# Seven block products for half of the up tiles, two unit queues merged by readiness, and loads without staging copies

## The chip, the core and the metric

The kernel runs on one core of one Trainium2 chip. The metric is the device time in microseconds (us) of one execution. Before the change it took 415.5 us (median of 4 runs, 415.48 to 416.22). A core has TensorE (the matmul engine, PE in the profile; PEld is its weight loads), VectorE (DVE), ScalarE (ACT), GpSimd (POOL) and SyncE (SP), which each take their instructions in order, and DMA queues that move data.

The kernel is built by a program that keeps a **plan**: for every instruction it works out when it would start and end, from fixed durations, and it orders the instructions of all engines by these times. The plan prints nothing, but its times can be read while it orders. They are its own estimates and not measurements. Below, "the plan ends at 408.2" is such a time, and "drift" is the start of a matmul in the trace minus its start in the plan. "Before" and "after" are used as the names of the two kernels.

## The reference, cut to what matters

```python
batch, n_q_heads, n_kv_heads, seq, head_dim = (8, 16, 4, 384, 64)
n_tokens, d_model, d_ff = (3072, 1024, 2048)

def reference(q, k, v, w_in, w_out):
    scores = matmul(q, k.T) / sqrt(64)          # 4 query heads share one kv head
    o = matmul(softmax(scores), v)
    x = o.transpose(0, 2, 1, 3).reshape(3072, 1024)
    h = maximum(x @ w_in, 0.0)                  # "up": 1024 -> 2048, then squared
    return (h * h) @ w_out                      # "down": 2048 -> 1024
```

Each batch gives 384 tokens. For one batch, up is 16 tiles of 128 columns of d_ff by 384 tokens. Down is already done in 2x2 blocks by 7 products in place of 8 (sums of operands before, sums of results after) in both kernels.

## The kernel before

Nearly every matmul is cut into pieces of 64 rows of the contraction. Two such pieces run side by side in the two halves (row groups) of the array. Both halves of a unit add into the same PSUM bank, so the second half may start only when the first is through. The plan's clock, with its two constants:

```python
SEM = 60.0       # an end is seen by another instruction 60 ns later
DRAIN = 190.0    # a matmul's result is there 190 ns after its columns

def add(self, eng, fn, reads, writes, ..., ns, rows, end):
    t = max([self.idle_at[eng]] + [self.ops[d]["end"] + self.SEM for d in need])
    if eng == "tensor":
        groups = (0, 1) if rows is None else (rows,)
        free = max([self.idle_at[eng]] + [self.rows_at[x] for x in groups])
        t = max(t, free)
        self.idle_at[eng] = t
        for x in groups:
            self.rows_at[x] = t + ns
        done = t + ns + self.DRAIN
    ...
```

The second half of a unit is held back, in row group 1 always, by a fixed 450 ns from the start of the last piece of its first half:

```python
GAP = 450.0
def hold_back(hi, last, done, frees=()):
    job = dict(hi=list(hi), ready=R.ops[last]["start"] + GAP, after=[last], ...)
    behind.append(job)
```

One up tile is 8 + 8 pieces of 384 columns; an attend unit (softmax weights by v) is 18 + 18 pieces of 65 columns:

```python
def row_up(b, c, then=None, final=False):
    i = yield from next_bank()
    def piece(h, kc):
        rows = ROWS[h]
        return Piece(h, 162.5, lambda pe: pe.matmul(acc[:, 0:S],
            w_in_sb[rows, kc, c * 128:(c + 1) * 128], xT[b % NXT][rows, kc, :], ...))
    def done():          # VectorE: relu out of PSUM; then ScalarE: square
        ...
    lo, hi = ([piece(h, kc) for kc in range(NKC)] for h in range(2))
    yield from push("up", lo, hi, done)
```

Keys and values of the next batch come into staging tiles by rows of 3 x 64 elements, and GpSimd copies them into place:

```python
def load_k(b, after=(), end=None):
    R.add("gpsimd", lambda g: g.dma_start(k_st..., k[b].rearrange("g (p j) d -> p g (j d)", j=NJ)), ...)
def dup_all_k(b, eng="vector"):      # each key twice, side by side
    R.add(eng, lambda e: e.tensor_copy(k_dup[1][:, :, :, :], src.to_broadcast([128, HKV * NJ, 2, D])), ...)
```

The softmax here doesn't subtract the row's maximum and nothing guards it: scores larger than these inputs give would overflow.

Of the kernel before, what the change touches and what calls it, by code (L numbers as in the profile page):

```python
# [9 lines left out]
class Recorder:  # L10
# [6 lines left out]
    def __init__(self, nc):  # L17
        self.nc = nc
        self.ops = []
        self.writer = {}  # L20
        self.readers = {}
        self.dma_sems = {}
        self.dma_last = {}
        self.idle_at = dict.fromkeys(self.ENGINES, 0.0)
        self.rows_at = [0.0, 0.0]
        self.stalled = {}
# [3 lines left out]

    def needs(self, eng, reads, writes, dma=None, after=()):
        deps = set()
# [9 lines left out]
        for d in deps:  # L42
            o = self.ops[d]
            if o["dma"] is None and o["eng"] == eng and dma is None:
                if eng in self.IN_ORDER or d not in raw:
                    continue
            need.add(d)
# [5 lines left out]
    def add(self, eng, fn, reads=(), writes=(), dma=None, after=(), ns=500.0, lat=2200.0, rows=None, end=None):  # L53
        i = len(self.ops)
        need = self.needs(eng, reads, writes, dma, after)
# [81 lines left out]
def bass_gqa_attention__then__ffn_squared_relu_kernel(  # L137
# [23 lines left out]
    NEX, NXT, NHR, NY, NO, NS = 3, 3, 3, 6, 4, 5  # L161

    R = Recorder(nc)

# [4 lines left out]
    warm = sb("warm", [128, 256])  # L169
# [10 lines left out]
    k_st = sb("k_st", [128, HKV, NJ, D])  # L180
    v_st = sb("v_st", [128, HKV, NJ, D])
    k_dup = [a_late[:, 0:2 * NKV].rearrange("p (a x d) -> p a x d", a=HKV * NJ, x=2), sb("k_dup1", [128, HKV * NJ, 2, D]).ap()]
    EARLY_W = [("q_f", c) for c in range(NPB)] + [("k_f", g) for g in range(HKV)] + ["v_f"] + [("q_st", 0, c) for c in range(NPB)]
    EARLY_A = [("k_dup", 0, g, j) for g in range(HKV) for j in range(NJ)]
    q_st = [q_b0, q_next.ap()]
    v_aug = [sb(f"v_aug{i}", [128, HKV * NJ, D + 1]) for i in range(2)]
    kT = [sb(f"kT{i}", [128, HKV, S]) for i in range(2)]
    qT = [sb(f"qT{i}", [128, NPB, S]) for i in range(2)]
    expT = [sb(f"expT{i}", [128, 2 * NJ, S]) for i in range(NEX)]
    rinv = [sb(f"rinv{i}", [128, NJ, 2], f32) for i in range(2)]  # L190
    o_sb = [sb(f"o_sb{i}", [128, NJ, 2, D]) for i in range(NO)]
    xT = [sb(f"xT{i}", [128, NKC, S]) for i in range(NXT)]
    w_in_sb = sb("w_in_sb", [128, NKC, FF], f16)
    w_out_sb = sb("w_out_sb", [128, NFC, F], f16)
    hr = [sb(f"hr{i}", [128, S], f32) for i in range(NHR)]
    h2T = [sb(f"h2T{i}", [128, NFC, S]) for i in range(2)]
    y_sb = [sb(f"y_sb{i}", [128, F // 2], f32) for i in range(NY)]

# [8 lines left out]
    def load_k(b, after=(), end=None):  # L207
        R.add("gpsimd", lambda g: g.dma_start(
            k_st.ap().rearrange("p g j d -> p g (j d)"),
            k[b].rearrange("g (p j) d -> p g (j d)", j=NJ)),  # L210
            writes=["k_st"], dma="k", after=after, ns=900.0, lat=LOADS, end=end)

    def load_v(b, after=(), end=None):
        R.add("gpsimd", lambda g: g.dma_start(
            v_st.ap().rearrange("p g j d -> p g (j d)"),
            v[b].rearrange("g (p j) d -> p g (j d)", j=NJ)),
            writes=["v_st"], dma="v", after=after, ns=900.0, lat=LOADS, end=end)
# [9 lines left out]
    def load_w_in(i):  # L227
# [3 lines left out]
            writes=[("w_in", i)], dma=f"wi{i}", end=20500.0 + 2700.0 * i)  # L231
# [13 lines left out]
    def first_q(c0, c1):  # L245
# [14 lines left out]
    R.add("vector", lambda e: e.memset(warm[:], 0.0), writes=["warm"])  # L260
# [3 lines left out]
        pattern=[[-1, 128]], channel_multiplier=1), reads=["ident"], writes=["ident"])  # L264
    for i in range(2):
        R.add("gpsimd", lambda e, i=i: e.memset(v_aug[i][:, :, D:D + 1], 1.0), writes=[("v_one", i)])
# [5 lines left out]
    def dup_k(g, eng, j0=0, j1=NJ):  # L272
        src = k_f[:, g, j0:j1].unsqueeze(2).to_broadcast([128, j1 - j0, 2, D])
        R.add(eng, lambda e: e.tensor_copy(k_dup[0][:, g * NJ + j0:g * NJ + j1], src),
              reads=[("k_f", g)], writes=[("k_dup", 0, g, j) for j in range(j0, j1)])
# [43 lines left out]
    def turn_bank(banks):  # L319
        i = banks[slots[0] % len(banks)]  # L320
        slots[0] += 1
        if i >= 5:
            return f_ps[i - 5].ap().bitcast(bf16)[:, 0:S], ("f_ps", i - 5)
        return sc_bf[:, i, 0:S], ("sc", i)

    def turn_on_pe(src, src_keys, dst, dst_keys, banks, eng="vector", n=NJ):
        ps, key = turn_bank(banks)

        def tr(pe):
            for t in range(n):  # L330
                m = pe.matmul(ps[:, t * 128:(t + 1) * 128], src[:, t * 128:(t + 1) * 128], ident[:],  # L331
# [3 lines left out]
        R.add("tensor", tr, reads=[*src_keys, "ident"], writes=[key])  # L335
# [4 lines left out]

    def first_kT(g, b=0, banks=RING, j0=0, j1=NJ):
        turn_on_pe(k_dup[b][:, g * NJ + j0:g * NJ + j1].rearrange("p a x d -> p (a x d)"),
                   [("k_dup", b, g, j) for j in range(j0, j1)], kT[b][:, g, j0 * 128:j1 * 128],
                   [("kT", b, g, j) for j in range(j0, j1)], banks, n=j1 - j0)

    def first_qT(c, b=0, banks=RING):
        turn_on_pe(q_st[b][:, 2 * c:2 * c + 2, :].rearrange("p h e -> p (h e)"), [("q_st", min(b, 1), c)],
                   qT[b][:, c], [("qT", b, c)], banks)

    def first_oT(c, banks=RING, eng="vector"):  # L350
        turn_on_pe(o_sb[c % NO].ap().rearrange("p i s d -> p (i s d)"), [("o_sb", c % NO, x) for x in range(2)],
                   xT[0][:, c], [("xT", 0, c)], banks, eng)

    def dup_all_k(b, eng="vector"):
        src = k_st.ap().rearrange("p g j d -> p (g j) d").unsqueeze(2)
        R.add(eng, lambda e: e.tensor_copy(
            k_dup[1][:, :, :, :], src.to_broadcast([128, HKV * NJ, 2, D])),
            reads=["k_st"], writes=[("k_dup", 1, g, j) for g in range(HKV) for j in range(NJ)], ns=1500.0)

    def turn_k(b, g):  # L360
        gs = slice(g * NJ, (g + 2) * NJ)
        R.add("sync", lambda e: e.dma_start_transpose(
            kT[b % 2][:, g:g + 2].rearrange("p g (j c) -> p (g j) c", j=NJ),
            k_dup[1][:, gs].rearrange("p a x d -> p (a x d)")),
            reads=[("k_dup", 1, x, j) for x in (g, g + 1) for j in range(NJ)],
            writes=[("kT", b % 2, x, j) for x in (g, g + 1) for j in range(NJ)], dma=f"kt{b % 2}_{g}", ns=1250.0)

    def turn_q(b, c):
        cs = (c, c + 1)
        R.add("sync", lambda e: e.dma_start_transpose(  # L370
            qT[b % 2][:, c:c + 2, :].rearrange("p h (t c) -> p (h t) c", t=NJ),
            q_st[1][:, 2 * c:2 * c + 4, :].rearrange("p h e -> p (h e)")),
            reads=[("q_st", 1, x) for x in cs], writes=[("qT", b % 2, x) for x in cs],
# [9 lines left out]
    def prepare_v(b):  # L383
        R.add("gpsimd" if b > 1 else "vector", lambda e: e.tensor_copy(
            v_aug[b % 2][:, :, 0:D], v_st.ap().rearrange("p g j d -> p (g j) d")),
            reads=["v_st"], writes=[("v_aug", b % 2)])

    def operands(p):
        b, c = p // NPB, p % NPB
        return kT[b % 2][:, c // 2], qT[b % 2][:, c], [("qT", b % 2, c)], [("kT", b % 2, c // 2, j) for j in range(NJ)]  # L390
# [18 lines left out]
    def attend(p, s, alone=False):  # L409
        b, g = p // NPB, (p % NPB) // 2  # L410
        acc, acc_key = (po_alt, ("sc", 1)) if alone and s == 1 else (po_v, "po")

        def av(pe):
            for i in range(NJ):
                f = NJ * s + i
                for j in range(NJ):
                    m = pe.matmul(acc[:, i, s, :], expT[p % NEX][:, 2 * j + f % 2, f // 2 * 128:f // 2 * 128 + 128],  # L417
                                  v_aug[b % 2][:, g * NJ + j, :], start=(j == 0), stop=(j == NJ - 1))
# [14 lines left out]
    def put_x(p):  # L433
# [4 lines left out]
            reads=[("o_sb", p % NO, x) for x in range(2)], writes=[("xT", b % NXT, c)], dma=f"xt{p % 8}", ns=1250.0)  # L438

    GAP = 450.0  # L440
    START = 30000.0
    behind = []
# [22 lines left out]
    def hold_back(hi, last, done, frees=()):  # L465
        job = dict(hi=list(hi), ready=R.ops[last]["start"] + GAP, after=[last], done=done, over=False, frees=frees)
        behind.append(job)
        return job

    def next_hi():  # L470
        job = behind[0]
        op = job["last"] = job["hi"].pop(0).emit(job["after"])
        job["after"] = ()
        if not job["hi"]:
            behind.pop(0)
            job["over"] = True

            def finish():
                free.extend(job["frees"])
                if job["done"]:  # L480
                    job["done"]()

            at(R.ops[op]["end"], finish)
# [5 lines left out]
    def push(kind, lo, hi, done=None, prev=None, frees=()):  # L489
        if prev is not None:  # L490
            yield from wait(lambda: prev["over"])
        after = [prev["last"]] if prev is not None else ()
        for piece in lo:
            if piece.test:
                yield from wait(piece.test)
            last = yield kind, piece, after
            after = ()
        return hold_back(hi, last, done, frees)

    ROWS = (slice(0, 64), slice(64, 128))  # L500
    F_BANKS = [(sc_ps[:, 3], ("sc", 3)), (sc_ps[:, 4], ("sc", 4)), (f_ps[0].ap(), ("f_ps", 0)), (f_ps[1].ap(), ("f_ps", 1))]
    free = [0, 1, 2, 3]

    def next_bank():
        yield from wait(lambda: free)
        return free.pop(0)

    exped, scaled = set(), {NPB - 1}
    voiced = {1}
    turned, usable, upped = {}, {0}, set()  # L510

    def row_scores(p, half):
        kt, qt, keys, k_keys = operands(p)
# [8 lines left out]
        def over(last):  # L522
            def exp():
# [9 lines left out]
        return [piece(i) for i in range(3)], over, lambda: before in exped and parts <= prepared  # L533

    def row_attend(p, then=None):
        b, g = p // NPB, (p % NPB) // 2

        def piece(r, f, j):
            rows = ROWS[r]
            return Piece(r, 33.0, lambda pe: pe.matmul(  # L540
                po_v[:, f % NJ, f // NJ, :], expT[p % NEX][rows, 2 * j + f % 2, f // 2 * 128:f // 2 * 128 + 128],
                v_aug[b % 2][rows, g * NJ + j, :], start=(r == 0 and f == 0 and j == 0), stop=(r == 1),
                skip_group_check=True),
                [("expT", p % NEX, 2 * j + f % 2), ("v_aug", b % 2), ("v_one", b % 2)], ["po"])

        def done():
            rinv_v = rinv[p % 2].ap().unsqueeze(3)
            R.add("vector", lambda e: e.reciprocal(rinv_v, po_v[:, :, :, D:D + 1]),
                  reads=["po"], writes=[("rinv", p % 2)], ns=200.0)
            op = R.add("vector", lambda e: e.tensor_tensor(o_sb[p % NO][:, :, :, :], po_v[:, :, :, 0:D],  # L550
                                                           rinv_v.to_broadcast([128, NJ, 2, D]), ALU.mult),
                       reads=["po", ("rinv", p % 2)], writes=[("o_sb", p % NO, x) for x in range(2)], ns=560.0)
# [7 lines left out]
            if turned[b] == NPB:  # L560
                usable.add(b)
# [3 lines left out]
        lo, hi = ([piece(r, f, j) for f in range(2 * NJ) for j in range(NJ)] for r in range(2))  # L565
# [625 lines left out]
```

## Time and profile before

| | before |
|---|---|
| time, median of 4 | 415.5 us |
| PE, DVE, ACT, POOL busy | 406.9, 216.1, 216.2, 53.7 us |
| first split piece starts, last one ends | 31.8, 409.6 us |
| the plan's end | 413.2 us |

Two more lines of the same page: the slices of the DMA engines (40 slices of 10.4 us, busy tenths) and the queue of the loads (packets, MB, share of 16 engines):

```profile
DMA  8999995657859841966029960698112210020012
...
q0 software_dynamic: 34288, 16.65, 31.8%
```

### The profile page before, as it was taken

Reading aid. Unit: us, or ns where it says so; the run is one execution under the profiler, and the core shown is the slowest. Engines: PE = TensorE matmul, PEld = TensorE weight load, DVE = VectorE, ACT = ScalarE, POOL = GpSimd, SP = SyncE. Lnnn points to the kernel's source line nnn. Section 1 sums busy time; section 2 is a strip of 40 time slices with the busy share of each in tenths; the row PEclk is TensorE's granted clock in tenths of the full one; section 3 lists DMA queues with packets and bytes.
Section 4 is the critical chain, followed back from the end, with each engine's and each line's share of the span. In section 5 each row is a group of like instructions: output and inputs, shape, how many; then the busy total and the mean of one; then the engine's idle time right before and its main releaser. Section 6 shows DMA issues by size and latency. Waiting matters only on the chain.

```text
span 414.2 us, 13446 instructions
## 1 busy us (share of the span) xinstructions
PE 406.9 (98%) x6129; PEld 312.3 (75%) x6129; DVE 216.1 (52%) x480; ACT 216.2 (52%) x282; POOL 53.7 (13%) x68
## 2 busy tenths in 40 slices
PE   7999999999999999999999999999999999999997
PEld 4656776777767888778876799778877786788774
DVE  2664551469845466246556445535655446435553
ACT  4885762775655564655645466655664453213200
POOL 5852211041012000300003000300000000000000
PEclk9999999999999999999999999999999999999999
DMA  8999995657859841966029960698112210020012
GB/s 231 198 197 202 208 202 86 122 71 96 143 142 158 182 69 29 113 142 119 21 60 141 181 135 13 56 179 152 17 47 97 98 47 11 2 103 2 27 77 103
DMA packets 93353, 44.26 MB, mean 107 GB/s; under 512 B 71664, under 2 KB 87280, under 8 KB 93296
## 3 DMA queue, kind: packets, MB, share of 16 engines
q0 software_dynamic: 34288, 16.65, 31.8%
q1 hardware_dynamic: 55968, 24.49, 27.6%
q10 hardware_dynamic: 3040, 2.26, 1.8%
q8 instruction: 48, 0.79, 0.8%
q14 instruction: 9, 0.07, 0.1%
HBM read 35.65 MB, written 12.58 MB: 116 GB/s over the span
## 4 chain that ended last, share of the span: by engine, by line
PE 94%; DMA 3%; DVE 2%; ACTq 0%; issue 0%; ACT 0%; POOL 0%; DVEq 0%
PE f_ps L630 20%; PE sc_ps L630 17%; PE f_ps L794 16%; PE sc_ps L794 15%; PE po L540 12%; PE sc_ps L519 6%; PE sc_ps L688 2%; DMA w_late<-in_q_dram 2%; PE f_ps L688 2%; PE po L417 1%; PE sc_ps L400 1%; DMA xT<-o_sb 1%; DVE o_sb L430 1%; PE sc_ps L331 0%; PE f_ps L331 0%; PE sc_ps L577 0%
## 5 line engine op out<-in xcount | busy, mean ns | idle before, releaser
L630 PE MATMUL f_ps<-xT,w_in_sb 64*128 64x384 bf16 x1040 | 171.6, 322 | 0.0
L630 PE MATMUL sc_ps<-xT,w_in_sb 64*128 64x384 bf16 x992 | 168.9, 323 | 0.2 <-DMA xT<-o_sb 0.2
L524 ACT ACTIVATE expT<-sc_ps 128x1152 bf16<-128x1152 f32 x110 | 124.2, 1129 | 81.2 <-PE sc_ps L519 55.3
L630 PEld LDWEIGHTS f_ps<-xT,w_in_sb 64*128 64x128 f16 x1040 | 89.8, 94 | 14.3
L649 ACT ACTIVATE h2T<-hr 128x384 bf16<-128x384 f32 x121 | 62.4, 520 | 67.7 <-DVE hr L641 67.0
L630 PEld LDWEIGHTS sc_ps<-xT,w_in_sb 64*128 64x128 f16 x992 | 87.8, 94 | 12.3 <-DMA xT<-o_sb 0.3
L540 PEld LDWEIGHTS po<-v_aug,expT 64*128 64x128 bf16 x2016 | 78.1, 94 | 15.1 <-DVE o_sb L550 2.0
L540 PE MATMUL po<-v_aug,expT 64*128 64x65 bf16 x2016 | 85.0, 190 | 0.0
L794 PE MATMUL f_ps<-w_out_sb,h2T 64*128 64x512 f16 x240 | 60.5, 376 | 0.0
L794 PE MATMUL sc_ps<-w_out_sb,a_late 64*128 64x512 f16 x240 | 59.8, 376 | 0.0
L519 PE MATMUL sc_ps<-qT,kT 64*128 64x384 bf16 x330 | 56.3, 323 | 0.0
L794 PE MATMUL sc_ps<-w_late,h2T 64*128 64x512 f16 x224 | 55.9, 376 | 0.0
L641 DVE TENSOR_SCALAR hr<-f_ps 128x384 f32<-128x384 f32 x65 | 36.1, 556 | 36.7 <-PE f_ps L630 27.0
L641 DVE TENSOR_SCALAR hr<-sc_ps 128x384 f32<-128x384 f32 x62 | 34.2, 556 | 35.6 <-PE sc_ps L630 21.4
L702 DVE TENSOR_TENSOR y_sb<-sc_ps,y_sb 128x512 f32<-128x512 f32 (+1 forms) x31 | 21.2, 687 | 47.1 <-PE po L540 23.4
L550 DVE TENSOR_TENSOR o_sb<-po,rinv 128x384 bf16<-128x384 f32 x56 | 31.2, 557 | 1.9
L794 PE MATMUL f_ps<-w_late,a_late 64*128 64x512 f16 x128 | 32.1, 376 | 0.0
L794 PE MATMUL f_ps<-w_late,h2T 64*128 64x512 f16 x128 | 31.8, 376 | 0.0
L519 PEld LDWEIGHTS sc_ps<-qT,kT 64*128 64x128 bf16 x330 | 24.5, 94 | 6.8 <-ACT expT L524 0.4
L794 PEld LDWEIGHTS sc_ps<-w_out_sb,a_late 64*128 64x128 bf16 x240 | 22.1, 94 | 4.8 <-PE f_ps L794 0.3
L794 PEld LDWEIGHTS f_ps<-w_out_sb,h2T 64*128 64x128 bf16 x240 | 21.5, 94 | 5.4 <-PE f_ps L630 0.2
L794 PEld LDWEIGHTS sc_ps<-w_late,h2T 64*128 64x128 bf16 x224 | 20.5, 94 | 6.0 <-PE sc_ps L794 0.2
(104 smaller groups left out, 407.8 us busy)
## 6 DMA issues: line engine op xcount, KB each, us to landing
out_dram<-y_sb SPq DMA_DIRECT2D x47, 256.0 KB, 2.5
q_next<-in_q_dram POOLq DMA_DIRECT2D x7, 768.0 KB, 11.3
w_in_sb<-in_moe_w_in_dram POOLq DMA_DIRECT2D x8, 512.0 KB, 11.8
w_out_sb<-in_moe_w_out_dram POOLq DMA_DIRECT2D x2, 2048.0 KB, 32.1
k_st<-in_k_dram POOLq DMA_DIRECT2D x7, 192.0 KB, 4.6
v_st<-in_v_dram POOLq DMA_DIRECT2D x7, 192.0 KB, 11.8
w_late<-in_q_dram ACTq DMA_DIRECT2D x1, 768.0 KB, 9.8
xT<-o_sb SPq DMA_TRANSPOSE x48, 2.6
```

Source lines behind the costliest of these rows:

```text
L400: m = pe.matmul(sc_ps[:, 2 * u + x, 0:S], kt[rows, j * 128:(j + 1) * 128], qt[rows, :])
L417: m = pe.matmul(acc[:, i, s, :], expT[p % NEX][:, 2 * j + f % 2, f // 2 * 128:f // 2 * 128 + 128], v_aug[b % 2][:, g * NJ + j, :], start=( ...
L519: return Piece(x, 162.5, lambda pe: pe.matmul(sc_ps[:, i, 0:S], kt[rows, j * 128:(j + 1) * 128], qt[rows, :]), keys + k_keys[j:j + 1], [(" ...
L524: R.add("scalar", lambda e: e.activation(expT[p % NEX][:, 3 * half:3 * half + 3, :], sc_ps[:, 0:3, 0:S], AF.Exp, scale=0.125), ns=1130.0, ...
L540: return Piece(r, 33.0, lambda pe: pe.matmul(po_v[:, f % NJ, f // NJ, :], expT[p % NEX][rows, 2 * j + f % 2, f // 2 * 128:f // 2 * 128 + 128],
L550: op = R.add("vector", lambda e: e.tensor_tensor(o_sb[p % NO][:, :, :, :], po_v[:, :, :, 0:D], rinv_v.to_broadcast([128, NJ, 2, D]), ALU.m ...
L630: return Piece(h, 162.5, lambda pe: pe.matmul(acc[:, 0:S], w_in_sb[rows, kc, c * 128:(c + 1) * 128], xT[b % NXT][rows, kc, :], start=(h == ...
L641: op = R.add("vector", lambda e: e.tensor_scalar_max(hr[r][:, :], acc[:, 0:S], 0.0), reads=[key], writes=[("hr", r)], ns=560.0)
L649: op = R.add("scalar", lambda e: e.activation(h2T[b % 2][:, c, :], hr[r][:, :], AF.Square), reads=[("hr", r)], writes=h2(b, c), ns=520.0)
L688: return Piece(h, 216.0, lambda pe: pe.matmul(acc, h2T[b % 2][rows, c, i * 128:(i + 1) * 128], w_out_sb[rows, c, jj * 512:(jj + 1) * 512], ...
L702: return R.add("vector", lambda e: e.tensor_tensor(out_ap, a, b, op), reads=reads, writes=writes, ns=ns)
L794: return Piece(h, 216.0, lambda pe: pe.matmul(acc, lhs[rows], right[rows, c], start=(first and h == 0 and c == 0), stop=(h == 1 and c == N ...
```

## The change

Its intent is to take columns off TensorE, which the profile shows as the limit. It has four parts.

1. For batches 2 to 7, two of four column groups of up (8 of 16 tiles) are computed in 2x2 blocks by 7 products of 192 columns.
2. Up and down units come from two queues. Whichever is ready first is taken, by either row group.
3. The sums of w_in which these products need are made by VectorE, one at a time behind those of w_out.
4. GpSimd only loads: keys (twice) and values go straight into place, by rows of 64 elements.

The diff is 1,629 lines long; this is its core, with cuts marked:

```diff
-    NEX, NXT, NHR, NY, NO, NS = 3, 3, 3, 6, 4, 5
+    NEX, NXT, NY, NO, NS = 2, 2, 8, 4, 6
+    UPG = (0,1,)
 ...
     def load_k(b, after=(), end=None):
-        R.add("gpsimd", lambda g: g.dma_start(
-            k_st.ap().rearrange("p g j d -> p g (j d)"),
-            k[b].rearrange("g (p j) d -> p g (j d)", j=NJ)),
-            writes=["k_st"], dma="k", after=after, ns=900.0, lat=LOADS, end=end)
+        for x in range(2):
+            R.add("gpsimd", lambda g, x=x: g.dma_start(
+                k_dup[1][:, :, x, :], k[b].rearrange("g (j p) d -> p (g j) d", j=NJ)),
+                writes=[...], dma=f"k{x}", after=after, ns=900.0, lat=LOADS, end=end)
 ...
-    GAP = 450.0
-    START = 30000.0
+    START = 31800.0
 ...
-    def hold_back(hi, last, done, frees=()):
-        job = dict(hi=list(hi), ready=R.ops[last]["start"] + GAP, after=[last], ...)
+    def second_half(r, make, last, unit):
+        later[r].append(dict(pieces=make(r, True), ready=R.ops[last]["end"] + R.SEM, after=[last], unit=unit))
 ...
+    def x_sums(b, which):
+            if n == 1:
+                op = tensor_op(x_sum[s1], A21, A22, ALU.add, ...)
+            if n == 2:
+                op = tensor_op(x_sum[s2], x_sum[s1], A11, ALU.subtract, ...)
 ...
+    def all_u_sums(todo, behind=()):
+        if todo:
+            op = u_sums(*todo[0], behind=behind)
+            at(R.ops[op]["end"] + USPACE, lambda: all_u_sums(todo[1:]))
 ...
+    def up_product(q, n, bank, first, done, prev=None, frees=()):
+        def piece(h, second, e, kc):
+            return Piece(h, 82.5, lambda pe: pe.matmul(bank.acc[:, e * HT:(e + 1) * HT], w[rows], x[rows], ...))
+        parts = [lambda r, second: [piece(r, second, e, kc) for e in range(2) for kc in range(KH)]]
 ...
+    streams = [up_stream(), down_stream()]
+    requests = [next(x) for x in streams]
 ...
+        for r in range(2):
+            for job in later[r][:3]:
+                t = max(job["ready"], job["pieces"][0].begin(job["after"]))
+                choices.append((t, job["unit"]["age"], r, "later", job))
```

## The prediction

> **What bounds the kernel now.** I read the page first, then busy time by stretch, then the timeline of one dense stretch to get the price of one instruction.
>
> ```profile
> PE 406.9 (98%) x6129; PEld 312.3 (75%) x6129; DVE 216.1 (52%) x480; ACT 216.2 (52%) x282; POOL 53.7 (13%) x68
> PE 94%; DMA 3%; DVE 2%; ACTq 0%; issue 0%; ACT 0%; POOL 0%; DVEq 0%
> ```
>
> The first line is busy time by engine, the second the chain that ended last. Both name TensorE, but matmuls overlap, so "98% busy" could hide slack. The stretches:
>
> ```profile
> 31.80:72.00 40.20, 39.96 (x731) 29.03 (x732) 18.50 (x44) 21.44 (x26) 9.16 (x10) 1.00 1.13 174
> 72.00:112.00 40.00, 40.00 (x674) 30.32 (x670) 28.07 (x59) 27.95 (x36) 5.47 (x5) 1.00 0.71 103
> ...
> 232.00:272.00 40.00, 40.00 (x634) 33.79 (x632) 20.80 (x48) 24.33 (x33) 4.96 (x5) 1.00 0.58 90
> ```
>
> (Columns: length, PE, PEld, DVE, ACT, POOL busy, clock, DMA share, GB/s.) TensorE has work from 31.8 us to 412 us, the clock is full, and VectorE and ScalarE are half idle except at 72 to 112 us (70%). How much of that is real work the timeline shows. All work after 31.8 us, except the last product, is in 64-row pieces, two row groups side by side:
>
> ```profile
> 56.15 0.33 PE L630 MATMUL f_ps<-xT,w_in_sb 64*128 64x384 bf16 x1
> 56.16 0.32 PE L540 MATMUL po<-v_aug,expT 64*128 64x65 bf16 x5
> 56.31 0.32 PE L630 MATMUL f_ps<-xT,w_in_sb 64*128 64x384 bf16 x1
> 56.33 0.32 PE L540 MATMUL po<-v_aug,expT 64*128 64x65 bf16 x5
> 56.48 0.32 PE L630 MATMUL f_ps<-xT,w_in_sb 64*128 64x384 bf16 x1
> ```
>
> One row group starts a 384-column piece every 0.16 us (the listed 322 ns is latency), while the other starts five 65-column pieces in the same time, some 32 ns each. In another dense stretch the 512-column pieces start 0.216 us apart. The counts are from the groups by line:
>
> ```profile
> L630 PE MATMUL f_ps<-xT,w_in_sb 64*128 64x384 bf16 x1040 | 171.6, 322 | 0.0
> L630 PE MATMUL sc_ps<-xT,w_in_sb 64*128 64x384 bf16 x992 | 168.9, 323 | 0.2 <-DMA xT<-o_sb 0.2
> L540 PE MATMUL po<-v_aug,expT 64*128 64x65 bf16 x2016 | 85.0, 190 | 0.0
> L519 PE MATMUL sc_ps<-qT,kT 64*128 64x384 bf16 x330 | 56.3, 323 | 0.0
> ```
>
> Halved for two row groups: up 2032 x 162.5 ns / 2 = 165.1 us; scores 330 x 162.5 / 2 = 26.8; attends 2016 x 32 / 2 = 32.3; down (L794 and L688 in 512 columns, 1344 in all) x 216 / 2 = 145.2; transposes and the last full-height product about 3. Sum 372 us, against 412 - 31.8 = 380 us. So only some 8 us in the dense part are holes, about 3 of them at its two ends (the hand-over at 32 to 35 us, the unsplit last product). The kernel is bound by the number of TensorE columns. A better order can win 4 or 5 us at most; the rest must come from fewer columns.
>
> **What the Trainium skill says.** "TensorE: Matmul & The Clock Gate", section "Back-to-back issue gap", gives N/2.4 + 2.5 ns warm for a lone stream: 162.5 ns at 384 columns and 216 at 512, which this trace shows in each row group. It also gives about 131 ns at 512 as a sustained figure for streams with weight loads; no single row group here does that, so the measurement decides. Its section "LDWEIGHTS (loading the stationary operand)" gives columns/1.2, 107 ns for 128; the trace has 94 ns, and since attend pieces start every 32 ns, loads are pipelined and will not hold up pieces of 192 columns. "TensorEngine Tiling (Array Packing)", "PSUM Bottleneck", warns that tiling speeds TensorE but not the evacuation of PSUM: here DVE and ACT are at 52%, so there is room, but the change spends it. "DMA: Bandwidth & Descriptors", "Specifications", asks for at least 512 B per transfer for line rate; the change goes the other way.
>
> **The change part by part.**
>
> Up products. For batches 2 to 7 two of four column groups, 8 of 16 up tiles, are computed in 2x2 blocks by 7 products instead of 8. Removed: 6 x 8 tiles x 16 pieces x 162.5 ns / 2 = 62.4 us. Added: 12 groups x 7 products x 16 pieces of 192 columns, by the same formula 82.5 ns each, / 2 = 55.4 us. Net **-7.0 us**, all on the path (an eighth of the columns, 7.7 us, less 0.7 us for 2.5 ns on 576 more pieces). TensorE's matmuls go up by 12 x 112 - 768 = 576.
>
> VectorE. Per group 4 relus of 556 ns become 7 sums of 384 columns (a 384-column PSUM operation took 557): 3 x 0.556 x 12 = +20 us. Sums of x: 6 x 4 x about 0.55 (768 columns, between the 424 measured for 512 and 681 for 1024) = +13. Sums of w_in: 8 x 0.69 = +5.5. In the down products seven copies move from ScalarE to VectorE sums (7 x 0.69 = +5) and ten products no longer share a bank, one more sum each (+7). About 216 + 50 = 266 us, 65%.
>
> ScalarE. Per group 4 squares become 1 copy + 4 relus + 4 squares: 5 x 0.52 x 12 = +31; minus 7 x 0.58 = -4. About 243 us, 60%. Neither engine becomes the bound, but results come out of TensorE in 0.66 us halves and their answers queue up, so local waits get likelier.
>
> GpSimd. Six key copies (1467 ns) and six value copies (906 ns) go: -14 us of POOL, none of it on the chain. In place, keys are loaded twice, straight into the doubled layout, and row order changes so that rows are 64 elements and not 192: per batch 512 packets become 3072 for k and 512 become 1536 for v. The loads' queue is busy until about 65 us (the slices show the DMA at 8 to 9 tenths up to 60 us), and batch 2's q and k are at its end, behind w_in and w_out. Two batches' worth of keys and one of values before them is 6144 more small packets. The queue's mean is 31.8% x 16 x 414.2 us / 34288 = 61 ns per packet, with about 1.5 in flight per engine; for a row of 128 B I estimate a half or less, so some 5 to 9 us later. Before, batch 2's first scores started at 75 us, some 10 us after its q had landed. In the change the plan keeps its landing times (62, 67 us), only the start of the plan moves from 30 to 31.8 us, where the trace has it. So I expect **0 to 4 us** of stall near 72 to 78 us; I take +1. In steady state a load is issued some 45 us before it is needed: nothing.
>
> Order. Two queues (up, down) merged by readiness, a fifth PSUM bank in the pool, either row group may start a unit. This goes for the 4 or 5 us of scattered holes. But seven shorter units with sums between them make new ones, there are two xT and expT buffers in place of three, and VectorE and ScalarE now wait for themselves on reused buffers also. I take **-0.5 us** net.
>
> Prologue (31.8 us) and tail: VectorE loses 0.9 us of copies there, GpSimd gains about 1.2 us of load issue against a wait of 1.1 us just behind it. I take 0; the last product is the same.
>
> Sum: 415.5 - 7.0 + 1 - 0.5 = 409.0. Since the order was evidently tuned for this mix, I lean a little lower: **408.5 us**.
>
> **The rivals.** (1) The merge removes most of the scattered holes: -3 more, near 405. For it: three 40 us stretches show no PE idle at all, so such density is possible. Against: the holes are already small, and PE busy cannot show those in one row group. (2) The sums take the place of the removed work: products wait for VectorE, at 75% or more around 66 to 112 us where w_out and now w_in sums run. Then half of the gain goes back: 412. For it: +50 us of VectorE; against: mean load 65%, and two tiles plus two products need no sums. (3) The small packets delay batch 2 by the full 4 us or more, or w_out before its first use at 59 us (it landed near 50): 411 to 413. (4) The weight loads bind at 192 columns (94 ns > 82.5): +0.7 us at most per group if loads did not overlap, all the gain gone, about 415; the 32 ns attends speak against it.
>
> **Range and chances.** The certain part is -7.0 us (1.7%), just under the 2% line (407.2 us), which needs 1.3 us more from the order than the new waits cost. I put 8 in 10 on 404.5 to 412.5, a bit over a third on faster by 2%, very little on slower.
>
> **What would show it.** Right: 1344 pieces of 192 columns, starting 82 to 83 ns apart in a row group; about 365 us of row-group work after 31.8 us; DVE near 265 us, ACT near 243, POOL near 40; PE's dense part ending near 405. Wrong: pieces of 192 columns more than 90 ns apart; PE idle of more than 2 us in a row near 70 to 80 us, released by the k or q load or its transposes; PE idle released by VectorE sums; a prologue that ends later than 33 us; or a dense part with under 3 us of holes, which would make it faster than 405.

## More of the kernel before

The DMA engines are nearly full up to 60 us (q, k, v and the weights come in). Then they have bursts every 35 to 50 us, when the next batch is loaded in one go.

## The result and the profile after

After took 413.1 us (median of 4 runs, 412.56 to 414.35), before 415.51 us in the same rounds. The ratio is 0.9942, with a 95% interval of 0.9917 to 0.9967. All ratios here are the mean time of one kernel's fast runs over that of the other's of the same rounds, so they are not quite the ratio of the medians. All runs of all kernels were fast (none over 1.5% above the fastest of its kernel). 408.5 us was predicted, with 404.5 to 412.5 as the range. The gain is 2.4 us and not 7.

The page of after (busy by engine, the loads' queue, the chain that ended last by engine, and one group of instructions with count, busy time and mean):

```profile
PE 403.0 (98%) x6705; PEld 306.8 (74%) x6705; DVE 256.3 (62%) x563; ACT 238.5 (58%) x335; POOL 50.0 (12%) x64
...
q0 software_dynamic: 59488, 18.02, 42.0%
...
PE 84%; DMA 11%; DVE 2%; POOL 1%; issue 1%; ACT 0%; ACTq 0%; DVEq 0%
...
L225 POOL DMA_DIRECT2D k_dup<-in_k_dram x14 | 14.4, 1039 | 180.9 <-DMA xT<-o_sb 180.9
```

There are 6705 matmuls, 576 more than the 6129 of before, as worked out. VectorE and ScalarE are near the estimates. The chain was 94% PE before and is 84% now; the 11% of DMA are mainly one long step that is read further down. The columns are gone as predicted. Here is a stretch with block products, in the timeline of TensorE in after (start, latency, instruction):

```profile
220.28 0.24 PE L891 MATMUL po<-xT,u_late 64*128 64x192 f16 x1
220.29 0.24 PE L891 MATMUL f_ps<-a_late,u_late 64*128 64x192 f16 x1
220.36 0.24 PE L891 MATMUL po<-xT,u_late 64*128 64x192 f16 x1
220.37 0.24 PE L891 MATMUL f_ps<-a_late,u_late 64*128 64x192 f16 x1
220.44 0.24 PE L891 MATMUL po<-xT,u_late 64*128 64x192 f16 x1
```

Here one row group writes to po and the other to f_ps. Each starts a piece every 0.08 us (82 to 83 ns in the records). So the piece of 192 columns costs what the formula said. The busy time by stretch of after (length, then PE, PEld, DVE, ACT, POOL busy, clock, DMA share, GB/s) shows something that was not there before:

```profile
200.00:240.00 40.00, 39.26 (x754) 33.98 (x752) 26.76 (x57) 26.36 (x38) 4.17 (x4) 1.00 0.82 109
240.00:280.00 40.00, 38.71 (x716) 32.42 (x714) 24.34 (x55) 25.90 (x36) 4.17 (x4) 1.00 0.85 117
```

Before had 40.00 of 40.00 for PE in both of these stretches. Now both row groups together stand still for 0.7 and 1.3 us. In one row group there is more, which this view cannot show, since the other group covers it. So I matched every split piece of the plan with its record in the trace, kernel by kernel, and added up, in each row group, the time between the end of a piece's columns (start plus 162.5 ns for 384 columns, and so on) and the start of the next. Gaps over 0.04 us, halved for two groups, are called **holes** here. "Holes planned" is the part of them that the plan has too, that is its own gap at those same places:

| kernel | first split piece | columns' work | holes planned | holes in the trace | last piece ends | time (median) |
|---|---|---|---|---|---|---|
| before | 31.8 | 370.5 | 4.4 | 8.0 | 409.6 | 415.5 |
| after | 31.0 | 363.4 | 4.0 | 13.8 | 407.9 | 413.1 |

This closes: -0.9 for the earlier first piece, -7.1 for the columns, +5.8 for holes make -2.2 us; the last piece ends 1.8 us earlier and the median is 2.4 us lower. **The columns were saved in full, and holes ate most of the gain.** The plan did not know of them: it ends at 408.2 us, and its drift grows from -0.9 us at the start to +5.6 us at the end. In before the drift grew by 0.65 us only. What follows is the search for the 5.8 us.

Three kinds of place are seen in after. **(A) Second halves of attend units.** The timeline of TensorE in after:

```profile
234.68 0.22 PE L622 MATMUL sc_ps<-v_aug,expT 64*128 64x65 bf16 x2
...
234.92 0.33 PE L891 MATMUL po<-a_late,w_in_sb 64*128 64x192 f16 x2
235.43 0.20 PE L622 MATMUL sc_ps<-v_aug,expT 64*128 64x65 bf16 x1 [0.16 <-PE f_ps L1099]
235.45 0.39 PE L1099 MATMUL f_ps<-w_out_sb,a_late 64*128 64x512 f16 x1
```

The first half of an attend (65 columns) ends with the two pieces of the first line, at 234.68 and 234.71. Its second half starts at 235.43, 0.7 us later. TensorE takes instructions in order, so the 512-column piece behind it, which belongs to the other row group, waits too, and nothing at all starts for 0.4 us. Over all second halves that stalled in after, the start came a median of 0.58 us after the last piece of the first half had started, where that piece has 65 columns (24 cases, 0.45 to 0.73). Where it has 384 columns it is 0.38 us (7 cases), with 512 it is 0.44 (7 cases). The plan says 0.28, 0.41 and 0.47. It is right on the long pieces and 0.3 us too early on the short ones. I count some 3.6 us of such stalls.

The kept trace also shows why. It holds the time of every update of TensorE's semaphore, the counter by which a piece tells others that it is done. In all 14 traces these updates are never less than 34 ns apart; in after, 64% of them follow the one before by 34 or 35 ns. A 384-column piece that finds no queue is counted 337 ns after its start, a 512-column one 390. But 1,948 of the 2,016 split pieces of 65 columns are counted, and together with those of the other row group they come faster than one in 34 ns, so their updates line up. Take for each length the time of an update without a queue (207 ns after the start at 65 columns, 256 at 192, 337 at 384, 390 at 512): a queue that lets one update through every 34 ns then gives 95% of the update times of after within 10 ns; without the queue it is 37%. In 21 of 23 stalls behind 65-column pieces (all those with a gap over 0.04 us) the second half starts 46 ns after the update of the last piece, and that update comes a median of 0.54 us after the piece's start. So the plan's 0.28 lacks this queue.

**(B) Holes in which TensorE waits for nothing that is shown.** The timeline of after again:

```profile
272.52 0.24 PE L891 MATMUL f_ps<-xT,u_late 64*128 64x192 f16 x1
272.53 0.25 PE L622 MATMUL po<-v_aug,expT 64*128 64x65 bf16 x3
274.05 0.19 PE L622 MATMUL po<-v_aug,expT 64*128 64x65 bf16 x1 [1.27 <-issue]
```

The hole lies in the middle of a run of 65-column pieces that need nothing new. A second one, of 0.82 us, is at 223.40. Both fall into the burst of a batch's loads. The trace also has the packets of the instruction queue: 16 KB each, 52 in after, for 13,470 recorded instructions of TensorE, so that a packet is a block of 256. I counted them against the instructions that TensorE had started. At the start of both holes TensorE had started 256 for each block whose packet began at least 2.3 us earlier, and 449 more, **to the instruction the same number**. It starts again when the next block's packet is 2.3 to 2.6 us old. So I call what is left of 256 per block plus 449 the **stock** of instructions, and it was 0 in both. In steady state a packet begins when the stock has come down to some 250; in the bursts of loads it begins late, at a stock of 63 to 131. Before has the same bursts, but TensorE takes fewer instructions per us there (longer pieces), and its stock was never under 60 after 65 us.

**(C) One-off waits.** The chain that ended last of after, in order of time (start, length, what):

```profile
33.15 35.55 DMA q_next<-in_q_dram
68.72 3.22 DMA qT<-q_next
71.99 0.49 PE sc_ps L592 x3
...
113.07 3.04 DMA xT<-o_sb
116.11 1.28 issue
117.40 0.56 DVE a_late L1016
```

Batch 2's q, issued at 33 us, landed in full only at 68.7 (65.9 before; k 63.9 and v 71.1, where before had 61.8 and 66.9). Its transposes and the first scores hang on it, and this one step is most of the chain's 11% of DMA. And near 120 us VectorE's sums of x, which take their turn in order, wait for the last transpose of batch 2; TensorE then stands still for 0.77 us.

### The profile page after: what moved, and what is told of

Read it like the earlier page. It is cut to its first block, busy times and chain, and to the rows that moved or that the text cites.

```text
span 412.5 us, 14760 instructions
## 1 busy us (share of the span) xinstructions
PE 403.0 (98%) x6705; PEld 306.8 (74%) x6705; DVE 256.3 (62%) x563; ACT 238.5 (58%) x335; POOL 50.0 (12%) x64
## 4 chain that ended last, share of the span: by engine, by line
PE 84%; DMA 11%; DVE 2%; POOL 1%; issue 1%; ACT 0%; ACTq 0%; DVEq 0%
PE f_ps L1099 12%; PE sc_ps L1099 12%; DMA q_next<-in_q_dram 9%; PE sc_ps L745 7%; PE sc_ps L891 6%; PE f_ps L745 6%; PE po L1099 6%; PE sc_ps L592 5%; PE f_ps L891 5%; PE f_ps L622 5%; PE po L745 4%; PE sc_ps L622 3%; PE po L891 3%; PE po L622 2%; PE sc_ps L997 2%; PE po L429 1%
## 5 line engine op out<-in xcount | busy, mean ns | idle before, releaser
L745 PE MATMUL sc_ps<-xT,w_in_sb 64*128 64x384 f16 x512 | 92.4, 323 | 0.0
L745 PE MATMUL f_ps<-xT,w_in_sb 64*128 64x384 f16 x464 | 87.8, 323 | 0.2 <-DVE y_sb L1311 0.2
L745 PE MATMUL po<-xT,w_in_sb 64*128 64x384 f16 x288 | 56.1, 323 | 0.0
L761 ACT ACTIVATE h2T<-y_sb 128x384 bf16<-128x384 f32 x73 | 37.9, 521 | 27.1 <-DVE y_sb L753 27.0
L745 PEld LDWEIGHTS sc_ps<-xT,w_in_sb 64*128 64x128 f16 x512 | 43.9, 94 | 6.5 <-PE sc_ps L745 0.2
L745 PEld LDWEIGHTS f_ps<-xT,w_in_sb 64*128 64x128 f16 x464 | 41.1, 94 | 4.7 <-DVE y_sb L1311 0.4
L1099 PE MATMUL f_ps<-w_out_sb,a_late 64*128 64x512 f16 x160 | 39.8, 376 | 0.0
L225 POOL DMA_DIRECT2D k_dup<-in_k_dram x14 | 14.4, 1039 | 180.9 <-DMA xT<-o_sb 180.9
L622 PEld LDWEIGHTS sc_ps<-v_aug,expT 64*128 64x128 bf16 x828 | 31.2, 94 | 6.4 <-PE po L745 0.9
L622 PE MATMUL sc_ps<-v_aug,expT 64*128 64x65 bf16 x828 | 34.8, 190 | 0.3 <-PE f_ps L1099 0.2
L622 PE MATMUL f_ps<-v_aug,expT 64*128 64x65 bf16 x792 | 32.9, 190 | 0.1
```

Of the source, the lines that this page charges most:

```text
L225: R.add("gpsimd", lambda g, x=x: g.dma_start(k_dup[1][:, :, x, :], k[b].rearrange("g (j p) d -> p (g j) d", j=NJ)), writes=[("k_dup", 1, g ...
L622: return Piece(r, 33.0, lambda pe: pe.matmul(place[1][:, f % NJ, f // NJ, :], expT[p % NEX][rows, 2 * j + f % 2, f // 2 * 128:f // 2 * 128 ...
L745: return Piece(h, (t1 - t0) / 2.4 + 2.5, lambda pe: pe.matmul(place.acc[:, t0:t1], w_in_sb[rows, kc, c * 128:(c + 1) * 128], xT[b % NXT][r ...
L761: op = R.add("scalar", lambda e: e.activation(h2T[b % 2][:, c, :], y_sb[y][:, 0:S], AF.Square), reads=[("y", y)], writes=h2(b, c), ns=520.0)
L1099: return Piece(h, (f1 - f0) / 2.4 + 2.5, lambda pe: pe.matmul(bank.acc[:, f0:f1], lhs[rows], right[rows, c, f0:f1], start=(first and not s ...
```

## The experiments

Twelve runs were made, all with 5 rounds but one with 3 (the control is after again, and the last is the fifth again). Kernels of one call share the runs of before (medians 415.97 for the first four, 416.16 for the next four, 416.33 for the last four). The rivals were: the plan's wrong hand-over (A); late instructions under bursts of loads (B); the load path's small packets or the missing copies; and the products themselves, by their shorter halves.

### The control

The changed kernel again, unchanged.

> The changed kernel unchanged, as the control on this chip: 412.5 to 414.4 us, and in its profile the same two holes in which TensorE waits for nothing that the profile shows (some 0.6 and 1.3 us, near 224 and 273 us) if they belong to the program and not to one execution.

Measured: 412.6 us (411.84 to 413.48), ratio 0.9900 [0.9862, 0.9937]. Holes in its trace: 12.9 us, last piece at 407.0. So repeats differ by about a microsecond. Holes of kind B were there again, at other places (1.33 us at 265.65, 0.78 at 272.41), and again TensorE had started 449 more than 256 per block at the start of each. They come and go with the run; the stalls of kind A stay where they are (the one at 235.0 is at 233.6 here).

### The plan told of the late hand-over (theory A)

```diff
-            done = t + ns + self.DRAIN
+            done = t + ns + self.DRAIN + (LAG if rows is not None and ns < 50.0 else 0.0)   # LAG = 240.0
```

> The kernel's own plan is told that a run of 65-column pieces ends 240 ns later (in the trace of the changed kernel what waits for such a run starts 0.45 to 0.58 us after its last piece starts, and the plan counts on 0.28). The plan gets 2.4 us longer (410.6 for 408.2). Theory A (these runs are planned too early, TensorE stops in order for 0.2 to 0.4 us some 17 times, 3.6 us in sum): those stops go, the drift between plan and trace falls by about 3.5 us, the time is 411.5 to 412.5. Theory B (the loads' small packets hold up TensorE): the drift stays, the time follows the plan, about 415. Theory C (sums on VectorE hold it up): also about 415.

Measured: 412.98 us (410.84 to 415.2), ratio 0.9897: no gain in the median, and the widest spread of all. The profiled run was the slowest, and shows why. Its drift stays between -0.7 and +1.0 us up to 132 us (its one large rise there, 1.5 us, is at 70 us; the run with both mends has it too and says what it is), so the plan now fits better. Then comes this in its timeline, and in the busy time by stretch (the clock is the third figure from the end):

```profile
132.46 0.44 PE L625 MATMUL sc_ps<-v_aug,expT 64*128 64x65 bf16 x9
134.78 0.20 PE L625 MATMUL sc_ps<-v_aug,expT 64*128 64x65 bf16 x1 [1.89 <-issue]
```

```profile
132.00:135.00 3.00, 1.11 (x29) 0.95 (x26) 0.09 (x1) 1.64 (x4) 0.00 (x0) 1.00 1.56 138
135.00:137.00 2.00, 2.00 (x27) 1.63 (x23) 0.75 (x2) 0.70 (x1) 0.00 (x0) 0.61 0.19 20
137.00:139.00 2.00, 2.00 (x28) 1.96 (x25) 0.55 (x1) 1.16 (x3) 0.00 (x0) 0.53 0.32 66
```

A hole of 2.1 us of kind B (stock 0, the last block 12.1 us behind the one before), again in the middle of a run, and after it 4 us at 0.61 and 0.53 of the clock: together some 3.6 us (the drift grows by 1.5 at the low clock), as much as A was worth. The plan itself also ends later (410.6 in place of 408.2), since true hand-overs leave fewer places to fill. So in this run B hid what the mend of A brought.

### "GpSimd only loads" undone

```diff
+    k_st = sb("k_st", [128, HKV, NJ, D])
+    v_st = sb("v_st", [128, HKV, NJ, D])
 ...      # loads by rows of 3 x 64 into k_st and v_st; GpSimd copies them as before
+            dup_all_k(b, "gpsimd")
```

> Only the part GpSimd-only-loads is undone: keys and values land once in rows of 384 B in a staging buffer, and GpSimd doubles and spreads them (1467 and 906 ns each), as in the kernel before. 1024 packets per batch in place of 4608; the plan's length is the same 408.2. Theory B: the two holes without a shown wait go, 411 us. Theory A or C: within 0.5 us of the control, the holes of a run of attends stay.

Measured: 412.67 us (411.95 to 412.86), ratio 0.9898: the same as the control. A batch's k and v now came in 1,024 packets and not 4,608, and holes of kind B were still there (0.84 us at 175.26 and 0.45 at 223.67, both at stock 0). So it is not the small packets that cost the time, and the missing copies gain nothing either, although with the copies back the first split piece comes 0.6 us later than in the control (31.7 against 31.1): this part of the change is worth zero within half a microsecond.

### No block products

```diff
-    UPG = (0,1,)
+    UPG = ()
```

> The changed kernel with no up tile in block products: new order, new loads, five banks, old arithmetic. Its plan is 412.3 us long from a start at 31.8, the plan of the kernel before 413.2 from 30.0, so 2.7 us shorter. Theory A (the new order is what is run with stops, products or not): drift of 3 to 5 us on top, 415.5 to 418, no gain over the kernel before. Theory C (the products and their sums make the stops): it runs as planned, 412 to 413, and the products bring nothing.

Measured: 414.79 us (414.34 to 415.06), ratio 0.9951 [0.9915, 0.9987]. With the columns back, the merged order and the loads alone are about 1 to 2 us better than before, and the control is 2.2 us better than this. So the products, in the kernel as it was changed, are worth 2.2 us of their 7.0. The trace has 8.0 us of holes, against 12.9 in the control. None is of kind B: a block of instructions lasts longer with longer pieces, though the stock went down to 21 in one burst.

### The loads of a batch spread (theory B)

```diff
-            for load in (load_k, load_q, load_v):
-                load(b + 1, [landed])
-            ready_at(b + 1)
+            todo = [load_k_part 0, load_k_part 1, load_q_part 0, load_q_part 1, load_v]
+            def go(x, a):
+                todo[x](a)           # each waits for the matmul issued at that moment
+                if x + 1 < len(todo):
+                    at(now() + 4500.0, lambda: go(x + 1, [latest matmul]))
```

> Only the loads of batches 3 to 7 change: the same bytes, but five smaller loads (k, k, half of q, half of q, v) issued 4.5 us apart behind a matmul of that moment, in place of four back to back. The plan stays 408.2 us. Theory D (TensorE runs out of fetched instructions: a 16 KB instruction fetch comes 10 to 12 us after the one before while a batch's loads run, and TensorE takes over 500 instructions in that time where block products are dense): gaps between fetches fall under 9 us in those stretches, the holes of 0.7 to 1.5 us without a shown wait go, 410.8 to 411.5 against 412.6 of the control. If the holes do not belong to the loads: 412.6, holes stay.

Measured: 411.68 us (410.83 to 413.24), ratio 0.9886. The gain over the control is small (0.9 us of medians, from two calls), but the trace is clear: between 65 and 330 us the stock is never under 45, and no hole of kind B is left. The plan ends at 408.2 as the control's does, and the drift grows by 3.3 us in place of 5.5. Between 85 and 330 us the gaps between fetches are 9.7 us at most, where the control has up to 13.6; under 9 was expected, and the time is just above the expected range.

### Hand-over and spread loads together

> Both mends together: the plan knows that runs of 65-column pieces end 240 ns later (plan 410.6 us), and the loads are spread. Theories A and D together: drift between plan and trace within 1 us at the end (control 4.7 from -0.7), 410.5 to 411.3, and little spread between runs (e1 without the spread had 410.8 to 415.2). If either is wrong, 412 or more.

The edit is the two above together. Measured: 410.99 us (410.52 to 411.23), ratio 0.9863 [0.9836, 0.9890]. This is 2 us below the run with the hand-over alone, its runs spread over 0.7 us in place of 4.4, and it beats both given kernels. It is 0.7 us below the run with spread loads alone, which is the correction of A by itself. The drift is -0.8 us at the start and -0.7 at the end. That the two agree is in part luck: in between it rises to +1.0 at 70 us and falls slowly after. The waits of TensorE and the busy time by stretch show what happens at 70 us, a wait that took the place of those removed:

```profile
PE sc_ps L608 <- DMA qT<-q_next: 1.5, 1, 1.5
```

```profile
69.00:73.00 4.00, 2.52 (x30) 1.59 (x28) 3.77 (x7) 1.84 (x3) 0.00 (x0) 1.00 1.08 160
```

TensorE has a hole of 1.8 us at 69.87. It waits for batch 2's q, which the plan believes to have landed at 67.0. In after the same wait was 0.3 us only, because its stalls of kind A had made TensorE late by then.

### The hand-over without products

> The kernel without block products (414.8 us, plan 412.3, drift 2.6 us, no hole without a shown wait) with the 240 ns. Plan 413.1. Theory A: the drift goes nearly all, 412.8 to 413.2, faster than e3 by some 1.7 us. Otherwise it follows the plan, 415.6.

The edit: no products, and the first diff. Measured: 413.41 us (412.86 to 414.74), ratio 0.9926. Without products the correction alone gains 1.4 us (1.0 by the two ratios, as the runs are of two calls; 1.7 was expected), although the plan with it ends 0.8 us later (413.1 against 412.3): the end's drift falls from +1.6 to -0.2 us and the holes in the trace from 8.0 to 5.2. This is the cleanest evidence for A, since there were no holes of kind B in either run (stock 6 at the least here). The hole at 70 us is here too (2.2 us).

### No loads for batches 3 to 7 (a wrong result)

```diff
-            for load in (load_k, load_q, load_v):
-                load(b + 1, [landed])
```

> Wrong result on purpose: the changed kernel without the loads of batches 3 to 7 (they attend over batch 2's data again); everything else is the same. Theory D: fetches come every 5 to 9 us throughout, no hole over 0.45 us without a shown wait, 410.8 to 411.5. If holes stay, the loads do not make them.

Measured (3 rounds): 410.93 us (410.53 to 411.99), ratio 0.9867; the result is wrong (batches 3 to 7 use batch 2's operands). No hole of kind B; the stock is never under 79 between 65 and 330 us. The median is 1.7 us under the control's; the figure is a rough one, and this profiled run began its split pieces 1.3 us later than the control's (its clock was at half from 11.0 to 14.4 us). The spread loads have about half of it.

### Batch 2's landings told as they are

```diff
-        for load, landed in ((load_k, 62000.0), (load_q, 67000.0), (load_v, 68500.0)):
+        for load, landed in ((load_k, 64000.0), (load_q, 69000.0), (load_v, 71000.0)):
```

> The corrected hand-over and the spread loads of the fifth run, and the plan told that batch 2's k, q and v land at 64, 69 and 71 us instead of 62, 67 and 68.5 (they landed at 63.6, 67.0 and 70.8, and the scores that need q came to TensorE after a hole of 1.7 to 2.2 us in all three runs with the corrected hand-over). If the hole is only the plan's late arrival and other work can be put there: plan end 409.7 us in place of 410.6, no hole over 0.5 us at 69 to 73 us, and about 409 to 410 us. If other work cannot fill it or it merely moves: 410.5 to 411.5, as the fifth run.

This is on top of the hand-over and the spread loads. Measured: 408.3 us (408.04 to 409.8), ratio 0.9811 [0.9788, 0.9834]. It is 2.1 us below the same kernel without this edit. That is more than the 0.9 us between the two plans' ends, and below the range that I expected: the hole of 1.7 us is gone. (The 67.0 of my expectation is not when the last part of q landed, which was 68.3 us in the fifth run; the 69 given to the plan fits that.) This kernel's chain by engine, and its busy time by stretch:

```profile
PE 95%; DVE 1%; POOL 1%; DMA 1%; issue 0%; ACT 0%; ACTq 0%; DVEq 0%
```

```profile
69.00:73.00 4.00, 4.00 (x50) 2.80 (x47) 3.77 (x7) 2.01 (x4) 0.00 (x0) 1.00 0.86 115
```

```profile
200.00:240.00 40.00, 40.00 (x765) 34.16 (x763) 25.63 (x53) 28.27 (x42) 4.78 (x5) 1.00 0.84 110
240.00:280.00 40.00, 40.00 (x777) 34.85 (x775) 27.41 (x61) 26.90 (x39) 4.77 (x5) 1.00 0.91 124
```

The DMA step is out of the chain, other up tiles fill 69 to 73 us, and PE is full where after had 38.71 of 40. The last stretch has 61 matmuls more than after had there (777 against 716), though not of the same units. It is the fastest kernel, about 1.9% under before.

### Half of the dose

```diff
-    UPG = (0,1,)
+    UPG = (0,)
```

> One column group in block products instead of two (4 of 16 up tiles, half of the dose), with the corrected hand-over and the spread loads. The columns removed are half, 3.5 us. If the products' gain is proportional to the columns: halfway between none and two. If the shorter halves eat it, as the corrected plan says (its end is 410.7 us here, 410.6 with two groups, 413.1 with none): this run equals the run with two groups within 0.5 us, about 411, so that the second group is worth nothing.

On top of the hand-over and the spread loads. Measured: 410.63 us (410.37 to 410.71), against 410.44 for two groups. **The second group of products is worth nothing measurable here** (0.2 us), though it takes 3.5 us of columns: the trace has 6.3 us of holes with one group and 10.3 with two. The plan had said so, once its hand-over was right (410.7 and 410.6). Neither half of the dose with the landings mended nor no products with these two mends alone was run, so this is shown only for kernels with the hole at 70 us.

### No products, with all the mends

> No block products, with everything else mended: corrected hand-over, spread loads, and the landings of batch 2 told as they are. Plan end 411.9 us. The best that the new order alone gives; against the run with products and the same mends it shows what the seven products are worth: 2 us by the two plans' ends (I expect 411.5 to 412.5 here), 7 us if the columns alone counted.

The edit: no products, the hand-over, the spread loads and the landings. Measured: 410.27 us (410.06 to 411.79), ratio 0.9863, 1.2 us better than the low end of what I had expected. The merged order alone, mended, takes 6.1 us off before. The block products then take off 2.0 more (410.27 to 408.30).

### The fifth kernel again

> The fifth run's kernel again, unchanged, for the comparison on the same chip and as a check of its result: 410.5 to 411.3 us, no hole that begins over 1 us after an instruction fetch that came 10 us or more behind the one before it.

Measured: 410.44 us (410.42 to 410.6), ratio 0.9855. The result repeats, and so does the trace: the hole at 70 us (1.7 us) and none of kind B.

### All together

The table of holes, for the runs that carry the argument (us; from each profiled run):

| kernel | columns' work | holes planned | holes in the trace | last piece ends | time (median) |
|---|---|---|---|---|---|
| before | 370.5 | 4.4 | 8.0 | 409.6 | 415.5 |
| after; its control | 363.4 | 4.0 | 13.8; 12.9 | 407.9; 407.0 | 413.1; 412.6 |
| no products | 370.4 | 1.7 | 8.0 | 407.8 | 414.8 |
| no products, hand-over | 370.4 | 2.2 | 5.2 | 406.9 | 413.4 |
| no products, all mends | 370.4 | 1.3 | 2.4 | 403.5 | 410.3 |
| products, spread loads | 363.4 | 4.1 | 10.5 | 404.7 | 411.7 |
| products, hand-over and spread loads; again | 363.4 | 6.3 | 10.3; 10.3 | 404.0; 403.9 | 411.0; 410.4 |
| products, all mends | 363.4 | 5.2 | 8.0 | 401.5 | 408.3 |

## Why the prediction was wrong

**Up products, net -7.0 us.** Right as far as it goes. 576 more matmuls, 82 to 83 ns between pieces, and 7.1 us less of columns' work. "All on the path" was right in the sense that every piece was. It was wrong in the sense that mattered: the gain that the products bring with everything else mended is 2.0 us, because the holes grow from 2.4 to 8.0 us with them.

**VectorE about 266, ScalarE about 243, GpSimd about 40.** Measured 256.3, 238.5 and 50.0. Neither became the bound, as said. GpSimd was 10 us off since the issue of the added key loads counts as busy (14 of 1,039 ns); it cost nothing.

**Loads: "0 to 4 us of stall near 72 to 78 us; I take +1".** The mechanism was right and its size within the range: q landed 2.8 us later than before. In after only 0.3 us of it showed, since TensorE had lost time elsewhere. In every run with the hand-over mended and the landings not, it was a hole of 1.6 to 2.2 us at 70 us.

**Order: "-0.5 us net".** This is the step that failed. In its place the runs show +5.8 us of holes from before to after, made of parts that nearly cancel in my sum and do not on the chip.

- The order itself gains more than I gave it. Without products and with a plan that fits the chip better, holes fall from 8.0 to 2.4 us. I had put 4 or 5 us as the most that an order can win; this is 5.6.
- The products open as many again, 5.6 us (2.4 to 8.0, both mended). "Seven shorter units with sums between them make new ones" is in the text, but it was sized at under 4 us. Half of a product is 8 pieces of 82.5 ns, 0.66 us. By what ended the holes, those that end with a result of TensorE's own (for a second half, its first half) go from 0.45 to 2.44 us, and those that end with VectorE from 0.8 to 2.2. The rest of the growth (0.95 to 3.8) is in holes before pieces whose own needs had ended earlier; what held these up is not shown.
- The other 5.8 us (13.8 in after, 8.0 with the mends) come from what the plan did not know: the hand-over of short pieces (A: semaphore updates that queue up at 34 ns each), late instructions (B), and q's landing. The three mends together bring the control from 412.6 to 408.3 us. One at a time they bring 0 (the hand-over, hidden by B), 0.9 (the spread loads), 1.6 (both) and then 2.1 more (only the last within one call), so their shares depend on the order in which they are mended.

I had no line for this third kind. The diff showed the change of `start + GAP` to `end + SEM`, that is from 450 to 283 ns behind a short piece. I passed over it. The trace of before would have told me: in it too, second halves that stalled behind a run of short pieces came a median of 0.58 us behind its last one (11 cases). A plan with 450 was nearer to that than one with 283.

**Prologue and tail, 0.** The first split piece comes 0.9 us earlier, since VectorE's copies of keys and values are gone (with them back it came at 31.7 us, near before's 31.8).

**The rivals.** (1) The order removes holes: true, and hidden. (2) The sums take the place: true in part (holes that VectorE ends grow by 1.4 us), but 412 was reached by another way. (3) The small packets: right about q, wrong about the rest; undoing them changes nothing (412.67). (4) Weight loads at 192 columns: wrong, pieces start 82 to 83 ns apart.

The predicted number, 408.5, is nearly that of the kernel with the three mends (408.3). This is luck and no merit: the order and loads, mended, give -6.1 where I had +0.5 for both, and the products -2.0 where I had -7.0.

**What stays open.** For B it is shown that all eight such holes of 0.45 us or more, in four runs, begin at a stock of exactly 0, that no other hole over 0.4 us does, and that spread or no loads keep the stock up and end them. How a load delays the fetch of instructions, both being DMA, is not shown, nor why a block counts only 2.3 to 3.0 us after its packet began. For A, the queue of semaphore updates explains the 0.58 us, but a kernel with fewer counted pieces, which would mend the cause and not the plan, was not tried; why an update takes 34 ns is not shown. The fall of the clock after a hole was seen once in the dense part; that the hole caused it is not shown. The fastest kernel was profiled once, and I tried no other size for its three numbers (240 ns, 4.5 us, the landings) on the chip.

## What to carry to other kernels

When TensorE is bound by columns, saved columns are worth only what the order can close up behind them: work out the holes that shorter units open before counting the saving as gain, and try half the dose, for here, with the hole at 70 us in both, half did as well. If an order comes out of a plan, lay the plan beside the trace instruction by instruction; a drift that grows names the wrong duration, and mending the plan (hand-over, landings) together with spreading the loads brought more than the seven products did (4.3 against 2.0 us). A run of short pieces that each count a semaphore is done later than its columns say. Issue bulk loads in parts where instructions are short and dense.

## What the Trainium skill lacked or had wrong

- "Runtime: NRT & Kernel Launch", "Instruction fetch mechanics": blocks of 16 KiB and 256 instructions agree with this trace. The page also gives TensorE room for 2048 instructions and calls the crossing mostly hidden. But a note in the same section says that there are only two lines of 16 KiB, and this trace fits the note better: a fetch begins in steady state when some 250 are left. TensorE stood still for 0.45 to 2.1 us when a fetch came late. That bursts of loads delay the fetch is not on the page.
- How long after its last piece a run of matmuls can be followed by an instruction that needs its result: no page has a figure by length of piece. "TensorE: Matmul & The Clock Gate", "The cost: per-tile semaphore tail", has the mechanism: increments serialize, by its fit at 26.3 ns each. Here updates are never under 34 ns apart, and what follows starts a median of 0.58 us (0.45 to 0.73) after pieces of 65 columns, 0.38 after 384, 0.44 after 512.
- "TensorE: Matmul & The Clock Gate", "Back-to-back issue gap": the sustained 131 ns at 512 columns was not seen in a row group (216 ns). The formula that the page calls isolated, N/2.4 + 2.5, holds in dense streams with weight loads, at 192 columns too (82 to 83 ns).
- The same page, "HAM oscillation — how this bites in real kernels", warns of idle gaps over about 3.4 us. In one run the clock fell to 0.61 and 0.53 for 4 us after a gap of 2.1 us, and in the run without loads it was at half for 3.4 us in the prologue, after a gap of 1.6 us.
